# Smaller operand loads and a shared eviction in a talking-heads attention plus two-MoE-layer kernel

## The chip, the cores and the metric

The kernel runs on one core of a Trainium2 chip. The metric is the device time of one execution in microseconds (us), as a median of runs. Differences of under about 0.3% (2.2 us here) count as no change.

## The reference

Two batches, 12 heads, 448 positions, 64 values per head, all float32. Attention mixes its heads twice: the scores before the softmax with `w_pre`, the weights after it with `w_post`.

```python
scores = scale * np.matmul(q, k.transpose(0, 1, 3, 2))
scores = np.einsum('bhij,hg->bgij', scores, w_pre)
scores = scores - np.max(scores, axis=-1, keepdims=True)
attn = np.exp(scores)
attn = attn / (np.sum(attn, axis=-1, keepdims=True) + 1e-09)
attn = np.einsum('bhij,hg->bgij', attn, w_post)
return np.matmul(attn, v)
```

Its output, 896 tokens of 768 values, passes a gated layer (`g = x @ w_gate; x = silu(g) * (x @ w_val) @ w_out`, inner width 1536) and a second one (`h = x @ w_in; x = h * relu6(h + 3) / 6 @ w_out`, inner width 2048).

## The kernel before

The order of all work is written out by hand; nothing is scheduled by a planner. Within an engine instructions run in that order, and so do the DMA issues of a queue (SP's, except a few of ACT's at the start).

Attention works on **tiles** of up to 120 query positions, four per batch (t = 0 to 7), and inside a tile on **chunks** of 10 positions: 12, 12, 12, 9 and 11, 12, 12, 10 chunks, 90 in all. Two chunks are a **pair**, and a pair is one **step** of the main loop at the kernel's end (i = 0 to 44). One step holds, in PE's order:

- `postmix(i)`: 64 small products of the softmax numerators `e` with the scaled weights `wn` into two PSUM tiles `ppost` (two buffers, so both are in use; the next `postmix` has to wait until both are evicted).
- `qk(t, c)`: the scores of one pair of heads for a tile that is needed later, into two PSUM tiles, evicted by `scores_out` (one by DVE, one by ACT) into the score tile `S`. A step holds one of these, steps 0 to 2, 15 and 17 two, and steps 37 to 44 none.
- `premix(i + 2)`: the mixing by `w_pre` of pair i + 2, from the tile `sx`.
- in 21 of the steps `av`: the products with the values of an earlier tile.

DVE takes the row maxima (`row_max`), ACT the exponentials (`exps`), DVE and POOL the weights `wn` (`weights`). `attn_out(i)` evicts the two `ppost` tiles into the tile `at`; before, ACT does both.

Between `qk` and `premix` the scores change their layout, from one head per plane to heads across partitions. That is the work of `relayout(m)`: for each chunk SP issues two DMAs from `S` to `sx`, one of 104 rows (182 KB) and one of 24 rows (42 KB), every row 1792 bytes long. A tile's chunks can only be relaid once all its scores are evicted; that is at the end of steps 2, 8, 14, 18, 24, 30 and 36 for tiles 1 to 7. Six chunks (fewer at step 18) are then issued at once, the others two per step.

On the same SP queue go the loads: query and key tiles of batch 1 (`load_q(1, ..)` and `load_k(1, ..)`, 1350 and 1344 KB, at the end of steps 4 and 5), the values (`load_v`, 1536 KB each: batch 0 ahead of the loop, batch 1 at step 8), and two weight pieces (`fetch`, 768 KB each, at steps 20 and 28). After the loop PE does the two layers without a break.

Of the kernel before, what the change touches and what calls it, by code (L numbers as in the profile page):

```python
# [18 lines left out]
DM = H * D  # L19
HP = H // 2  # L20
# [7 lines left out]
JC = 4  # L28
# [19 lines left out]
def kernel(  # L48
# [14 lines left out]
    nc = tc.nc  # L63
# [31 lines left out]
    qs, ks, vs = {}, {}, {}  # L95
# [5 lines left out]
    def load_q(b, i0, i1):  # L101
        lo, hi = (HP * KI * sum(c for _, _, c in TILES[b][:i]) for i in (i0, i1))
        nc.sync.dma_start(out=qs[b][:, lo:hi], in_=qT[b, :, lo:hi])

    def load_k(b, c0, c1, eng=nc.sync):
        eng.dma_start(out=ks[b][:, c0:c1, :], in_=kT[b, :, c0 * S : c1 * S].rearrange("p (c j) -> p c j", j=S))

    def load_v(b):
        vs[b] = pv.tile([128, JC, H, D], F32, name=f"v{b}", tag="v")
        nc.sync.dma_start(out=vs[b].rearrange("p c h d -> p (c h d)"), in_=vv[b])  # L110

    def load_q0(c0, c1, eng):
        n = TILES[0][0][2] * KI
# [7 lines left out]
    load_k(0, 2, 3)  # L121
    load_k(0, 3, 4, nc.scalar)
    load_k(0, 4, 5)
    load_k(0, 5, 6, nc.scalar)
    W1 = cst.tile([128, 64], F32, name="W1")
    W2 = cst.tile([128, H, KG], F32, name="W2")
    nc.scalar.dma_start(out=W1, in_=w_pre)
    nc.scalar.dma_start(out=W2.rearrange("p g k -> p (g k)"), in_=w_post)
    nc.gpsimd.tensor_scalar(W1, W1, 0.125, 1.0, ALU.mult, ALU.mult)
    load_q(0, 1, 4)  # L130

    Ss = [psc.tile([128, H + 1, S], F32, name=f"S{i}") for i in range(2)]
    for x in Ss:
# [48 lines left out]
    def relayout(m, small=nc.sync):  # L182

        t, c = chunks[m]
        b, i = divmod(t, 4)
        ncc = TILES[b][i][2]  # L190
        i, r = divmod(m, 2)
        if r == 0:
            sx[i] = psx.tile([128, 2, S], F32, name=f"sx{i}", tag="sx")
        rows = stiles[t][c : ncc * KI : ncc, :, :]
        nc.sync.dma_start(out=sx[i][0:104, r, :], in_=rows[:8, :, :])  # L195
        small.dma_start(out=sx[i][104:128, r, :], in_=rows[8:, :H, :])
# [3 lines left out]
    def premix(i):  # L200

        x = sx.pop(i)
        p = [ps.tile([128, 512], F32, name=f"ppre{i}_{a}", tag="ppre", bufs=BUFS["ppre"]) for a in range(2)]
        for r in range(2):
            for a in range(2):
                rows = slice(64 * a, 64 * a + 64)
                nc.tensor.matmul(  # L207
                    p[a][64 * r : 64 * r + 64, :S],
                    lhsT=W1[rows, :],
                    rhs=x[rows, r, :],  # L210
                    start=True,
                    stop=True,
                    tile_position=(64 * a, 64 * r),
                )
        for a in range(2):
            pre[2 * i + a] = p[a]

    def row_max(m):
        nm = pe.tile([128, 1], F32, name=f"nm{m}", tag="nm", bufs=6)
        nc.vector.tensor_reduce(nm, pre[m][:, :S], AX.X, ALU.max, negate=True)  # L220
        tot[m] = nm

    def exps(m):
        e = es[m % 6]
        sm = pe.tile([128, 1], F32, name=f"sm{m}", tag="sm", bufs=6)
        nc.scalar.activation(e[:, :S], pre.pop(m)[:, :S], AF.Exp, bias=tot.pop(m), scale=1.0, accum_out=sm)  # L226
        ew[m] = (e, sm)

    def weights(m):
        sm = ew[m][1]  # L230
        rc = pe.tile([128, 1], F32, name=f"rc{m}", tag="rc", bufs=6)
        nc.vector.tensor_scalar(rc, sm, 1e-9, None, ALU.add)
        nc.vector.reciprocal(rc, rc)  # L233
        wn = pe.tile([128, H, KG], F32, name=f"wn{m}", tag="wn", bufs=6)
        nc.gpsimd.tensor_scalar(wn, W2, rc, 1.0, ALU.mult, ALU.mult)  # L235
        wns[m] = wn

    def postmix(i):
        p = [
            ps.tile([128, 2, JC, H, KG], F32, name=f"ppost{i}_{s}", tag="ppost", bufs=BUFS["ppost"]) for s in range(2)  # L240
        ]
        for r in range(2):
            e, wn = ew.pop(2 * i + r)[0], wns.pop(2 * i + r)
            for b in range(JC):
                for c in range(2):
                    k0 = (2 * b + c) * JB
                    for s in range(2):
                        rows = slice(64 * s, 64 * s + GP)
                        nc.tensor.matmul(  # L249
                            p[s][64 * c : 64 * c + 64, r, b, :, :],  # L250
                            lhsT=e[rows, k0 : k0 + 64],
                            rhs=wn[rows, :, :],
                            start=True,
                            stop=True,
                            tile_position=(64 * s, 64 * c),
                        )
        post[i] = p

    def attn_out(i):
        p = post.pop(i)  # L260
        (t0, c0), (t1, c1) = chunks[2 * i], chunks[2 * i + 1]
        for t, c in ((t0, c0), (t1, c1)):
            if c == 0:
                ats[t] = pat.tile([128, JC, H, 120], F32, name=f"at{t}", tag="at")
        for r in range(2):
            if t0 == t1:
                dst = ats[t0][:, :, :, c0 * KI : (c0 + 2) * KI].rearrange("p b h (a k) -> p a (b h) k", k=KI)
                dst = dst[:, :, :, r * KG : (r + 1) * KG]
            else:
                t, c = chunks[2 * i + r]  # L270
                dst = ats[t][:, :, :, c * KI : (c + 1) * KI].rearrange("p b h (a k) -> p a (b h) k", k=KG)
            nc.scalar.copy(dst, p[r].rearrange("p a b h k -> p a (b h) k"))  # L272

    pavs, stage, xt = {}, {}, {}

# [154 lines left out]
    def halve(j):  # L430
        if j < len(subs):
            kind, idx, k0, kc, _ = subs[j]
            _, y, _ = ys.pop(j)
            pool = pools["wp0" if j < 2 else "wp"]
            whl[j] = split_w(pool, y, kc, f"{kind}{idx}_{k0}")
# [33 lines left out]
    for _ in range(8):  # L469
        relayout(placed, nc.scalar if placed < 4 else nc.sync)  # L470
        placed += 1
    load_v(0)


    extra = {i: {"qk": [], "av": [], "end": []} for i in range(-LOOK, NP)}

    def at_step(i, f, *args, place="end"):
        extra[i][place].append((f, args))

    def run(i, place):  # L480
        for f, args in extra[i][place]:
            f(*args)
# [15 lines left out]
    for t in range(7):  # L498
        begin = (first[t + 1] - 1) // 2 + 1
        end = first[t + 2] // 2 - 1 if t < 6 else NP - 1  # L500
        for c in range(HP):
            i = begin + (c // 2) * (end - begin) // 2
            at_step(i, av, t, c, place="av")
            at_step(i, x_out if t < 6 else x_last, t, c)
        if t < 6:
            step = 1 if t < 4 else 2
            i = split_at.setdefault(t, max(end + 1, split_at.get(t - 1, 0) + 4 // step))
            for part in range(4):
                at_step(i + part // step, x_split, t, part)
    at_step(4, new_qk, 1)  # L510
    at_step(4, load_q, 1, 0, 4)
    at_step(5, load_k, 1, 0, 6)
    at_step(8, load_v, 1)
    for b in range(2):
        at_step(scored[4 * b + 3] + 1, new_x, b)

# [7 lines left out]
    def fill(n):  # L524
        nonlocal fillers
        if fillers is None:
            fillers = first_products()
        for _ in range(n):
            next(fillers, None)

    for i in range(-LOOK, NP):
        if i >= 0:
            postmix(i)
        soft = [2 * (i + 1) + a for a in range(2)] if 0 <= i + 1 < NP else []
        for m in soft:
            exps(m)
        for m in soft[:1]:
            weights(m)
        run(i, "qk")
        for m in soft[1:]:  # L540
            weights(m)
        if i + LOOK < NP:
            premix(i + LOOK)
            for a in range(2):
                row_max(2 * (i + LOOK) + a)
        if i >= 0:
            attn_out(i)
        if i >= NP - 3:
            fill(FILL[i - NP + 3])
        run(i, "av")  # L550
        if i == 41:
            late.close()
            pools["wp0"] = ctx.enter_context(tc.tile_pool(name="wp0", bufs=2, side="right"))
        if i in (42, 43):
            halve(i - 42)
        run(i, "end")
        while placed < NCH and placed // 2 <= i + LOOK + 4 and i >= scored.get(chunks[placed][0], -3):
            relayout(placed)
            placed += 1
# [158 lines left out]
```

## Time and profile before

| | |
|---|---|
| median of 3 runs | 729.32 us (727.85 to 730.26) |
| profiled execution | 731.22 us, of which the span from first to last instruction is 729.4 us |
| mean granted TensorE clock | 0.988 of full speed |
| PE / DVE / ACT / POOL busy | 703.0 / 480.5 / 317.1 / 122.7 us |
| DMA | 86.66 MB, 119 GB/s on average |
| share of the chain that ended last | PE 86%, DMA 8%, ACT 3% |

The busy share of PE (96%) counts overlapped instructions and says little by itself. The chain, the gaps ahead of PE's instructions and the starts of the steps tell more. A row of the timeline reads: start, duration, engine, line, operation, output and inputs, count, and in brackets how long the engine had been idle and who ended that. PE is the matmul, PEld the weight load ahead of it, SPq the issue of a DMA by SP. Instructions on DVE and ACT overlap by some tenths, so the distance between two starts is what an instruction occupies.

### The profile page before, as it was taken

To read this page: it belongs to the slowest core of one execution; us is meant where nothing else is said; L and a number is where in the kernel's file an instruction comes from. 1 tells how busy PE (TensorE), PEld (TensorE's weight loads), DVE (VectorE), ACT (ScalarE), POOL (GpSimd) and SP (SyncE) were. 2 spreads that over 40 slices of the span, in tenths; PEclk is the share of its full clock that TensorE was granted. 3 is DMA by queue.
4 is the path that set the end of the run, shared out by engine and by line. 5 is a ranking of instruction groups with operands and counts; after the bars stand their busy time and mean duration, and the time that the engine had idled before them with its cause. 6 is when DMAs were issued, how large, how long until landed. Compare 5 with 4: busy or idle time off the path is not lost.

```text
span 729.4 us, 16450 instructions
## 1 busy us (share of the span) xinstructions
PE 703.0 (96%) x6864; PEld 580.7 (80%) x6864; DVE 480.5 (66%) x808; ACT 317.1 (43%) x608; POOL 122.7 (17%) x185
## 2 busy tenths in 40 slices
PE   8898989999999999999999999999999999999998
PEld 2354446565668999999999999999999999999997
DVE  2563455576751788888878766657888888665550
ACT  2573466687663443343333333224354453333230
POOL 0110112332151111311211100001323324000000
PEclk9898999999999999999999999999999999999999
DMA  5548322434231233333333423332233232544320
GB/s 208 177 153 258 115 78 100 153 127 162 102 114 73 87 126 101 120 122 106 119 93 124 130 88 102 118 127 87 87 102 116 86 123 81 175 143 137 117 90 26
DMA packets 26462, 86.66 MB, mean 119 GB/s; under 512 B 2708, under 2 KB 16788, under 8 KB 25876
## 3 DMA queue, kind: packets, MB, share of 16 engines
q1 hardware_dynamic: 25420, 84.44, 35.0%
q8 instruction: 54, 0.88, 0.5%
q10 hardware_dynamic: 968, 1.17, 0.5%
q14 instruction: 20, 0.16, 0.1%
HBM read 62.20 MB, written 2.75 MB: 89 GB/s over the span
## 4 chain that ended last, share of the span: by engine, by line
PE 86%; DMA 8%; ACT 3%; SPq 2%; issue 1%; POOL 0%; DVE 0%; ACTq 0%
PE pi L383 16%; PE pp L383 16%; PE po L383 12%; PE pg L383 12%; PE pv L383 12%; PE ppost L249 5%; PE pav L284 5%; DMA sx<-S 5%; PE pqk L162 4%; PE ppre L207 3%; ACT at L272 2%; DMA v<-in_v_dram 1%; ACT S L178 1%; PE p L383 1%; SPq L195 1%; DMA W<-in_w_pre_dram 1%
## 5 line engine op out<-in xcount | busy, mean ns | idle before, releaser
L383 PE MATMUL pp<-g,hp 128*128 128x448 f32 x384 | 109.1, 365 | 0.0
L383 PE MATMUL po<-u,ho 128*128 128x448 f32 x288 | 81.7, 364 | 0.0
L249 PEld LDWEIGHTS ppost<-wn,e 60*64 60x64 f32 x2880 | 53.8, 138 | 34.7 <-issue 23.2
L383 PEld LDWEIGHTS pp<-g,hp 128*128 128x128 f32 x384 | 71.9, 187 | 5.8
L249 PE MATMUL ppost<-wn,e 60*64 60x60 f32 x2880 | 62.4, 226 | 11.9 <-issue 5.6
L207 PE MATMUL ppre<-sx,W 64*64 64x448 f32 x360 | 65.0, 564 | 5.7 <-DMA sx<-S 5.7
L383 PE MATMUL pi<-x2h,li 128*128 128x448 f32 x192 | 70.2, 366 | 0.0
L579 POOL TENSOR_TENSOR g<-rl,g 128x448 fp32r<-128x448 f32 x32 | 41.5, 1318 | 169.0 <-ACT g L578 169.0
L383 PE MATMUL pi<-x2l,hi 128*128 128x448 f32 x192 | 70.0, 364 | 0.0
L383 PE MATMUL pi<-x2h,hi 128*128 128x448 f32 x192 | 69.9, 364 | 0.0
L383 PE MATMUL pp<-g,lp 128*128 128x448 f32 x192 | 69.3, 361 | 0.0
L220 DVE TENSOR_REDUCE nm<-ppre 128x1 f32<-128x448 f32 x90 | 52.5, 617 | 23.8 <-PE ppre L207 23.1
L226 ACT ACTIVATE e<-ppre,nm 128x448 f32<-128x448 f32 x90 | 56.5, 633 | 22.4 <-DVE nm L220 20.9
L178 DVE COPY S<-pqk 120x448 f32<-120x448 f32 (+3 forms) x48 | 30.0, 624 | 51.5 <-PE pqk L162 51.2
L579 POOL TENSOR_TENSOR u<-sg,u 128x448 fp32r<-128x448 f32 x24 | 32.7, 1380 | 151.3 <-ACT u L578 151.3
L383 PEld LDWEIGHTS po<-u,ho 128*128 128x128 f32 x288 | 54.1, 188 | 3.8
L162 PE MATMUL pqk<-k,q 64*64 64x448 f32 (+4 forms) x384 | 53.2, 555 | 3.4 <-ACT S L178 3.4
L235 POOL TENSOR_SCALAR wn<-W,rc 128x60 f32<-128x60 f32 x90 | 28.2, 314 | 163.1 <-DVE rc L233 101.7
L272 ACT COPY at<-ppost 128x480 f32<-128x480 f32 x90 | 52.8, 647 | 3.7 <-PE ppost L249 3.7
L383 PE MATMUL po<-u,lo 128*128 128x448 f32 x144 | 52.3, 363 | 0.0
L284 PEld LDWEIGHTS pav<-at,v 128*64 128x64 f32 x768 | 38.3, 140 | 16.3 <-ACT S L178 9.9
L383 PE MATMUL pv<-xl,hv 128*128 128x448 f32 x138 | 50.5, 366 | 0.0
(103 smaller groups left out, 1362.1 us busy)
## 6 DMA issues: line engine op xcount, KB each, us to landing
sx<-S SPq DMA_DIRECT2D x90, 182.0 KB
ri<-in_moe_w_in_dram SPq DMA_DIRECT2D x16, 768.0 KB
rg<-in_moe_w_gate_dram SPq DMA_DIRECT2D x12, 768.0 KB
rv<-in_moe_w_val_dram SPq DMA_DIRECT2D x12, 768.0 KB
ro<-in_moe_w_out_dram SPq DMA_DIRECT2D x12, 768.0 KB
rp<-in_moe_w_out_dram SPq DMA_DIRECT2D x12, 640.0 KB
rp<-in_moe_w_out_dram SPq DMA_DIRECT2D x6, 768.0 KB
sx<-S SPq DMA_DIRECT2D x86, 42.0 KB
```

Source lines behind the costliest of these rows:

```text
L162: nc.tensor.matmul(p[e][lo:hi, :S], lhsT=qs[b][r, base + lo : base + hi], rhs=ks[b][r, c, :], start=True, stop=True, tile_position=(64 * e ...
L178: copy(stiles[t][:n, h, :], pqk.pop((t, h))[:n, :S])
L195: nc.sync.dma_start(out=sx[i][0:104, r, :], in_=rows[:8, :, :])
L207: nc.tensor.matmul(p[a][64 * r : 64 * r + 64, :S], lhsT=W1[rows, :], rhs=x[rows, r, :], start=True, stop=True, tile_position=(64 * a, 64 * r),
L220: nc.vector.tensor_reduce(nm, pre[m][:, :S], AX.X, ALU.max, negate=True)
L226: nc.scalar.activation(e[:, :S], pre.pop(m)[:, :S], AF.Exp, bias=tot.pop(m), scale=1.0, accum_out=sm)
L235: nc.gpsimd.tensor_scalar(wn, W2, rc, 1.0, ALU.mult, ALU.mult)
L249: nc.tensor.matmul(p[s][64 * c : 64 * c + 64, r, b, :, :], lhsT=e[rows, k0 : k0 + 64], rhs=wn[rows, :, :], start=True, stop=True, tile_pos ...
L272: nc.scalar.copy(dst, p[r].rearrange("p a b h k -> p a (b h) k"))
L284: nc.tensor.matmul(p[64 * e : 64 * e + 64, :n], lhsT=vs[b][:, jc, h, :], rhs=ats[t][:, jc, h, :n], start=jc == 0, stop=jc == JC - 1, tile_ ...
L383: nc.tensor.matmul(p[:, :S], lhsT=wt[:, kk, :], rhs=xx, start=start, stop=stop)
L579: eng.tensor_tensor(to[1], src, to[0].bitcast(F32), ALU.subtract)
```

## The change

1. Loads of attention operands become small pieces. Values: four pieces of 384 KB per batch, one a step, for batch 0 at steps 1 to 4, for batch 1 at steps 17 to 20. Keys of batch 1: six pieces of 224 KB at steps 5 to 10. Queries of batch 1: four pieces of one tile each (300 to 360 KB) at steps 11 to 14. Queries of batch 0: tile 1 at the start as before, tiles 2 and 3 at steps 0 and 1. The last key piece of batch 0 goes from ACT's to SP's queue.
2. `attn_out` stands ahead of `weights`, `qk` and `row_max` in a step instead of behind them, and its first half goes to DVE, the second to ACT.

The order of PE's and of POOL's instructions stays the same.

```diff
+    def load_v(b, j):
+        nc.sync.dma_start(
+            out=vs[b][:, j].rearrange("p h d -> p (h d)"), in_=vv[b, :, j * DM : (j + 1) * DM]
+        )
...
-    load_k(0, 5, 6, nc.scalar)
+    load_k(0, 5, 6)
...
-    load_q(0, 1, 4)
+    load_q(0, 1, 2)
...
-            nc.scalar.copy(dst, p[r].rearrange("p a b h k -> p a (b h) k"))
+            copy = nc.scalar.copy if r else nc.vector.tensor_copy
+            copy(dst, p[r].rearrange("p a b h k -> p a (b h) k"))
...
-    load_v(0)
+    new_v(0)
...
-    at_step(4, new_qk, 1)
-    at_step(4, load_q, 1, 0, 4)
-    at_step(5, load_k, 1, 0, 6)
-    at_step(8, load_v, 1)
+
+    for n in range(2):
+        at_step(n, load_q, 0, 2 + n, 3 + n)
+    for j in range(JC):
+        at_step(1 + j, load_v, 0, j)
+    at_step(5, new_qk, 1)
+    for n in range(HP):
+        at_step(5 + n, load_k, 1, n, n + 1)
+    for n in range(4):
+        at_step(11 + n, load_q, 1, n, n + 1)
+    at_step(16, new_v, 1)
+    for j in range(JC):
+        at_step(17 + j, load_v, 1, j)
...
+        if i >= 0:
+            attn_out(i)
         for m in soft[:1]:
             weights(m)
         run(i, "qk")
...
-        if i >= 0:
-            attn_out(i)
```

On SP's queue, behind the first six chunks of tile 1 (the rows start with the last of them; `sx` is a relayout, `q`, `k`, `v` are loads), there stood in steps 3 to 5:

```order
L195 DMA sx_502<-S_108 104x1x448
L196 DMA sx_502<-S_108 24x1x448
L195 DMA sx_575<-S_108 104x1x448
L196 DMA sx_575<-S_108 24x1x448
L195 DMA sx_575<-S_108 104x1x448
L196 DMA sx_575<-S_108 24x1x448
L103 DMA q_648<-in_q_dram 128x2700
L195 DMA sx_651<-S_108 104x1x448
L196 DMA sx_651<-S_108 24x1x448
L195 DMA sx_651<-S_108 104x1x448
L196 DMA sx_651<-S_108 24x1x448
L106 DMA k_649<-in_k_dram 128x2688
```

In the changed kernel the same place on SP's queue reads:

```order
L199 DMA sx_505<-S_108 104x1x448
L200 DMA sx_505<-S_108 24x1x448
L112 DMA v_217<-in_v_dram 128x768
L199 DMA sx_579<-S_108 104x1x448
L200 DMA sx_579<-S_108 24x1x448
L199 DMA sx_579<-S_108 104x1x448
L200 DMA sx_579<-S_108 24x1x448
L112 DMA v_217<-in_v_dram 128x768
L199 DMA sx_653<-S_108 104x1x448
L200 DMA sx_653<-S_108 24x1x448
L199 DMA sx_653<-S_108 104x1x448
L200 DMA sx_653<-S_108 24x1x448
```

The two large loads between the pairs have gone, and the last two pieces of batch 0's values stand there in their place, behind four pairs of relayouts.

On DVE the step with the scores of head pair 3 of tile 2 (step 6; `rc` belongs to `weights`, `nm` is `row_max`) read:

```order
L232 TENSOR_SCALAR rc_768<-sm_764 128x1
L233 RECIPROCAL rc_768<-rc_768 128x1
L178 COPY S_107<-pqk_3_0_773 120x448
L232 TENSOR_SCALAR rc_781<-sm_766 128x1
L233 RECIPROCAL rc_781<-rc_781 128x1
L220 TENSOR_REDUCE nm_792<-ppre_0_786 128x1
L220 TENSOR_REDUCE nm_794<-ppre_1_787 128x1
```

On DVE the same step of the changed kernel reads:

```order
L277 COPY at_772<-ppost_0_734 128x2x48x5
L236 TENSOR_SCALAR rc_775<-sm_768 128x1
L237 RECIPROCAL rc_775<-rc_775 128x1
L182 COPY S_107<-pqk_3_0_780 120x448
L236 TENSOR_SCALAR rc_788<-sm_770 128x1
L237 RECIPROCAL rc_788<-rc_788 128x1
L224 TENSOR_REDUCE nm_799<-ppre_0_793 128x1
L224 TENSOR_REDUCE nm_801<-ppre_1_794 128x1
```

One eviction has come to DVE, ahead of everything else in the step. On ACT the step with the scores of head pair 5 of that tile read, exponentials first:

```order
L226 ACTIVATE e_111,sm_922<-ppre_0_876,nm_882 128x448
L226 ACTIVATE e_112,sm_924<-ppre_1_877,nm_884 128x448
L178 COPY S_107<-pqk_5_1_932 120x448
L272 COPY at_796<-ppost_0_888 128x2x48x5
L272 COPY at_796<-ppost_1_889 128x2x48x5
```

On ACT it now reads:

```order
L230 ACTIVATE e_111,sm_928<-ppre_0_883,nm_889 128x448
L230 ACTIVATE e_112,sm_930<-ppre_1_884,nm_891 128x448
L277 COPY at_772<-ppost_1_895 128x2x48x5
L182 COPY S_107<-pqk_5_1_940 120x448
```

The eviction left to ACT now stands ahead of the score eviction.

## Rows read from the trace of the kernel before

**Rows 1.** The chain of waits: start us, us, what (where the two layers begin).

```profile
237.19 3.84 PE pg L383 x18
```

**Rows 2.** The timeline of PE: steps 8, 12, 19 and 20.

```profile
58.36 1.09 PE L249 MATMUL ppost<-wn,e 60*64 60x60 f32 x59 [0.19 <-ACT at L272]
...
88.82 1.16 PE L249 MATMUL ppost<-wn,e 60*64 60x60 f32 x64
...
123.58 1.16 PE L249 MATMUL ppost<-wn,e 60*64 60x60 f32 x64
...
126.17 1.86 PE L284 MATMUL pav<-at,v 128*64 128x120 f32 x32
127.96 1.16 PE L249 MATMUL ppost<-wn,e 60*64 60x60 f32 x64
128.94 0.93 PE L162 MATMUL pqk<-k,q 64*64 64x448 f32 x8
129.69 0.93 PE L207 MATMUL ppre<-sx,W 64*64 64x448 f32 x8
...
131.62 1.09 PE L249 MATMUL ppost<-wn,e 60*64 60x60 f32 x59 [0.19 <-ACT at L272]
```

**Rows 3.** The timeline of the other engines at the end of step 20.

```profile
129.93 0.62 DVE L178 COPY S<-pqk 120x448 f32<-120x448 f32 x1 [1.31 <-PE pqk L162]
...
130.40 1.18 ACT L272 COPY at<-ppost 128x480 f32<-128x480 f32 x2
130.47 0.14 DVE L232 TENSOR_SCALAR rc<-sm 128x1 f32<-128x1 f32 x1
...
130.73 1.16 DVE L220 TENSOR_REDUCE nm<-ppre 128x1 f32<-128x448 f32 x2
130.98 0.31 POOL L235 TENSOR_SCALAR wn<-W,rc 128x60 f32<-128x60 f32 x1 [1.88 <-DVE rc L233]
```

**Rows 4.** The timeline of PE's weight loads: waits for relaid pairs.

```profile
44.44 0.19 PEld L207 LDWEIGHTS ppre<-sx,W 64*64 64x64 f32 x2 [0.22 <-DMA sx<-S]
...
52.01 0.19 PEld L207 LDWEIGHTS ppre<-sx,W 64*64 64x64 f32 x2 [0.49 <-DMA sx<-S]
...
177.67 0.19 PEld L207 LDWEIGHTS ppre<-sx,W 64*64 64x64 f32 x2 [0.69 <-DMA sx<-S]
...
181.28 0.19 PEld L207 LDWEIGHTS ppre<-sx,W 64*64 64x64 f32 x2 [0.63 <-DMA sx<-S]
...
201.22 0.19 PEld L207 LDWEIGHTS ppre<-sx,W 64*64 64x64 f32 x2 [0.68 <-DMA sx<-S]
...
205.10 0.19 PEld L207 LDWEIGHTS ppre<-sx,W 64*64 64x64 f32 x2 [0.72 <-DMA sx<-S]
...
216.34 0.19 PEld L207 LDWEIGHTS ppre<-sx,W 64*64 64x64 f32 x2 [0.67 <-DMA sx<-S]
```

**Rows 5.** The timeline of SP: issues at the pauses of the queue.

```profile
37.57 0.69 SPq L195 DMA_DIRECT2D sx<-S  x1
...
92.02 0.65 SPq L196 DMA_DIRECT2D sx<-S  x1
102.19 0.69 SPq L195 DMA_DIRECT2D sx<-S  x1
...
116.19 0.67 SPq L196 DMA_DIRECT2D sx<-S  x1
121.85 0.69 SPq L195 DMA_DIRECT2D sx<-S  x1
...
194.52 0.70 SPq L195 DMA_DIRECT2D sx<-S  x1
```

**Rows 6.** Stretches: us, busy PE PEld DVE ACT POOL, clock, DMA share, GB/s.

```profile
5.00:10.00 5.00, 4.96 (x48) 1.63 (x40) 3.06 (x5) 3.87 (x6) 0.00 (x0) 1.00 0.95 353
54.00:56.00 2.00, 2.00 (x84) 1.66 (x84) 0.78 (x4) 0.46 (x2) 0.31 (x1) 1.00 1.02 313
66.00:68.00 2.00, 2.00 (x13) 1.02 (x12) 1.25 (x2) 0.92 (x3) 0.00 (x0) 0.50 1.03 375
```

More of the change, by code (lines that the diff above doesn't have):

```diff
@@ L106, in load_k, with new_v @@
         eng.dma_start(out=ks[b][:, c0:c1, :], in_=kT[b, :, c0 * S : c1 * S].rearrange("p (c j) -> p c j", j=S))
-    def load_v(b):
+    def new_v(b):
         vs[b] = pv.tile([128, JC, H, D], F32, name=f"v{b}", tag="v")
-        nc.sync.dma_start(out=vs[b].rearrange("p c h d -> p (c h d)"), in_=vv[b])
+    def load_v(b, j):
+        nc.sync.dma_start(
+            out=vs[b][:, j].rearrange("p h d -> p (h d)"), in_=vv[b, :, j * DM : (j + 1) * DM]
+        )
     def load_q0(c0, c1, eng):
```

## The prediction, made before the change was run

> **What bounds the kernel now.** I read the chain of waits first, then PE's timeline step by step, then what PE's weight loads waited for, then SP's queue. The chain shows that the two layers begin at 237.19 us [rows 1], and from there hardly anything but PE is on it. Nothing in that stretch changes, so the forecast is about the first 237 us.
>
> The steps there are of two kinds. A step with value products (call it A) takes 127.96 - 123.58 = 4.38 us, of which these products are 127.96 - 126.17 = 1.79 us, and PE waits for nothing [rows 2]. A step without them (N) takes 131.62 - 127.96 = 3.66 us, though its work on PE is only 4.38 - 1.79 = 2.59 us: the next `postmix` waits for ACT, which evicts both `ppost` tiles last in its step, from 130.40 to 131.58 us [rows 2, 3].
>
> The second limit is the path of the relaid chunks; call it the conveyor. SP issues in order and the copies land in order. How fast they land shows where PE waits for pair after pair: the last copies of two pairs lie 52.01 - 44.44 = 7.57 us apart, those of neighbours 181.28 - 177.67 = 3.61 and 205.10 - 201.22 = 3.88 us [rows 4]. That is 15.06 us for four pairs, 3.76 us a pair and 1.88 us a chunk. SP issued the nine chunks of tile 3, 18 copies, from 102.19 to 116.19 us, about 1.6 us a chunk [rows 5]: the copies are moved more slowly than they are issued.
>
> So how full is the conveyor? From the first issue for tile 1 at 37.57 us to the last landing at 216.34 us [rows 4, 5] there are 178.8 us and 78 chunks: 78 x 1.88 = 146.6 us. Through the same queue go queries, keys and values of batch 1 and two weight pieces, 1350 + 1344 + 1536 + 2 x 768 = 5766 KB by the tiles' shapes; at 313 GB/s, the rate while two of them pass [rows 6], that is 18.9 us. The lead of the first pair is 44.44 - 37.57 - 3.76 = 3.1 us [rows 4, 5]. That leaves 178.8 - 146.6 - 18.9 - 3.1 = 10.2 us in which the conveyor stands still. They are found in SP's pauses: 92.02 to 102.19 and 116.19 to 121.85 us are two of them, the last ends at 194.52 us [rows 5], and of each some 4 us go to copies that are still landing. So this kernel alternates: first PE waits for loads and copies, then the conveyor waits for scores.
>
> A page of the Trainium skill, *DMA: Bandwidth & Descriptors*, section on why a DMA increments its semaphore by 16, says that such a DMA runs on as many of the 16 engines as divide the slowest dimension of both sides: by it the large copy (8 groups of 13 rows into 104) would use 8 engines, the small one (2 groups of 12 into 24) two of these. Two engines would then carry 25 of the 1792-byte rows of every chunk, 44.8 KB, which would explain a slow conveyor at a low mean share. At the page's 27 GiB/s an engine that would be, as an estimate, 1.5 us a chunk, and SP's issue would set the pace; the landings give 1.88, and the measurement decides.
>
> **The change, part by part.** *The eviction.* One `ppost` copy goes to DVE (480 elements; the `S` copy of 448 occupies 130.47 - 129.93 = 0.54 us [rows 3], so 0.58 us). The trace shows no DVE copy that writes runs of five elements; the bounds are 0.58 and twice that, 1.16 us, and I take 0.58, since the nearest row also reads PSUM. In an N step the chain becomes: `postmix` 128.94 - 127.96 = 0.98 us; the wake-up 129.93 - 129.69 = 0.24; the eviction 0.58; the first weights 130.73 - 130.47 = 0.26; the `S` copy 0.54; the second weights to the end of `wn` 131.29 - 130.47 = 0.82. That is 3.42 us, and the second half of the next `postmix` (0.49 us in) needs it, so N takes 2.9 to 3.0 us instead of 3.66 [rows 2, 3]. DVE's own load in it is 0.58 + 0.26 + 0.54 + 0.26 + 1.06 = 2.7 us, less than that. A stays at 4.38, because PE was not waiting there. Over 16 such N steps this is about 11 us of PE time, if PE sets the pace.
>
> *The large loads.* In before, queries, keys and values of batch 1 stand between the pairs of tile 1 and 2; from step 8 to step 12 PE needs 88.82 - 58.36 = 30.5 us [rows 2] for what is 4.4 + 3.7 + 3.7 + 5.4 = 17.2 us of work (tile 3's score products are slower). Spread out, these 4230 KB take the same 13.8 us of the conveyor; they are only no longer in one place. Two things get worse. First, two pieces of batch 0's values, 768 KB or 2.5 us, now go through the conveyor behind 37.57 us, ahead of which all of them went before. Second, the last of them stands behind four pairs of tile 1 on SP's queue, and step 6 needs it: 36.6 (start, below) + 3.1 + 4 x 3.76 + 2.5 = 57 us, while PE would be ready at about 51.5. PE will stand there for some 5 us and leave step 6 at about 58 us, 3 us later than before. The conveyor runs on meanwhile, so this costs the end little.
>
> *The start.* Less is loaded ahead of the first relayout, and steps 0 to 2, with two score products, each lose part of the wait for ACT: I take 1 us in all at the first issue for tile 1 (bounds 0 and 2.5), so 36.6 us. The key piece that changes queues lies ahead of the work that needs it: nothing.
>
> *The sum.* With PE faster in N steps and no block of loads, PE keeps ahead of the conveyor nearly everywhere, and the conveyor sets the end of attention. Between the issue points of two tiles it needs, with the pieces (0.7 us for a key piece, 1.25 for a value piece, 1.1 for a query piece): steps 3 to 8 28 us, 9 to 14 28.5, 15 to 18 19.4, 19 to 24 25.7 (with a weight piece), 25 to 30 25.1 (another), 31 to 36 22.6, and 18.8 for the last ten chunks. PE needs about 18, 27.4, 19.1, 23, 21.6 and 22.3 us for the six spans. The sum is 168 us; with 36.6 + 3.1 and 1.5 us for the start of tile 2's copies, which the wait in step 6 delays, the last pair lands at 209.3 us instead of 216.34. The gain is 7 us: 1.0 + 10.2 - 1.5 - 2.5. The 21 us from there to the layers stay. In the profiled execution's own time, 731.2 us, that is 724.2; it lies 1.9 us above the median of the runs, 729.3, so against these I forecast 722 us.
>
> Bounds: with 1.81 or 1.94 us a chunk (the closest and the widest pair) the idle time of before is 15.7 or 5.5 us and the gain 12.5 or 2.5 us, so 717 to 727.
>
> **The rivals.** *The conveyor is not the limit* (its pace follows SP's issues, and these follow PE). Then the steps' savings count in full: 11 us from N steps, 13 from steps 8 to 11, less 4 for the wait in step 6: 20 us, 709 us. For it: SP's pauses show that it had time. Against it: the three equal intervals, at times far apart.
>
> *PE falls behind after step 6.* After PE had waited for copies about 60 us, the granted clock from 66 to 68 us was 0.50, the lower of the two levels, 1.2 GHz [rows 6]; the wait in step 6 may do the same. If the next steps run so, tile 2's scores come 3 to 5 us later, the conveyor idles that long, and 3 us of gain remain: 726 us.
>
> *Small pieces hold the conveyor longer than their bytes* (slower). Sixteen pieces stand between relayouts. A copy of only 42 KB lands some 0.9 us after its large neighbour; were each piece to cost that much more than its bytes, it would be 14 us, and 736 us; from 0.45 us a piece on, the change loses. For it: these copies show that a small DMA is not cheap. Against it: from 5 to 10 us, where pieces of 224 KB and less were under way beside one large one, 353 GB/s were moved [rows 6]. The page named above, section Bandwidth, states the rule for this side: transfers should be batched to at least 1 MiB, with some 2 us fixed per DMA. If that were serial it would be, as an estimate, 32 us; the row speaks against it, since the fixed parts overlapped there.
>
> *The gains cancel* (a slower DVE eviction at 1.16 us makes N 3.5 us, and the conveyor idles as before): 729 us.
>
> **How the numbers follow.** Chances: the forecast 0.60, conveyor not the limit 0.13, PE behind 0.13, pieces slow 0.07, gains cancel 0.07. A measurement of this kernel tells 0.3%, 2.2 us, from no change, so faster means under 727.1. Faster: 0.59 of the forecast's, 0.13, and 0.08 of the third, 0.80; within 0.3%: 0.12; slower 0.08. The range of 8 in 10 runs from 712 to 728: it takes in the forecast's 717 to 727, the third case and the slower part of the second; what lies outside is most of 709, and 736.
>
> **What would show it.** Right: the layers begin at about 230 us; landings at 3.7 to 3.9 us a pair nearly without a pause from tile 1 on; PE waiting for `sx` in more steps than before, above all about steps 24 and 32; N steps of 2.9 to 3.0 us where no copy is awaited; no wait for ACT ahead of `postmix`; a wait of about 5 us for `v` in step 6. Wrong: a layers' begin at 217 us, or pairs that land faster than every 3.5 us, would show that the conveyor was no limit; windows with loads at well under 300 GB/s and pairs 5 us apart, that pieces are slow.

## The result, and the profile after

The changed kernel takes 721.98 us in the median (721.87 to 723.24), the kernel before beside it 728.59; the ratio is 0.991, with an interval of 0.989 to 0.994. A second set of runs gave 723.45 us and the same ratio, 0.991 [0.989, 0.993]. The forecast was 722 us, with 0.80 for faster.

| | before | after |
|---|---|---|
| profiled execution / span | 731.22 / 729.4 us | 721.89 / 720.0 us |
| the layers begin | 237.19 us | 227.07 us |
| first issue for tile 1 | 37.57 us | 35.43 us |
| last pair lands | 216.34 us | 207.11 us |
| conveyor stands still between the two | 7.8 us | 0.7 us |
| DVE / ACT busy | 480.5 / 317.1 us | 504.4 / 296.1 us |
| chain: PE / DMA / ACT / DVE | 86 / 8 / 3 / 0% | 88 / 4 / 3 / 3% |

The line on the standstill is counted from the packets' start times and durations: the stretches of over 0.3 us between those two times in which no packet of SP's queue was moving. In before it is the next three windows; the columns end with PE's clock, DMA's busy share and GB/s.

```profile
98.70:103.53 4.83, 4.81 (x102) 2.67 (x104) 2.66 (x8) 3.26 (x8) 0.63 (x2) 1.00 0.01 3
120.96:123.18 2.22, 2.22 (x40) 1.52 (x34) 1.99 (x6) 1.98 (x4) 0.74 (x2) 1.00 0.04 8
195.12:195.85 0.73, 0.73 (x19) 0.73 (x16) 0.73 (x3) 0.73 (x2) 0.10 (x1) 1.00 0.00 0
```

After, one is left. The second window here is the clock behind the wait for `v` in step 6.

```profile
65.20:65.93 0.73, 0.73 (x20) 0.73 (x16) 0.73 (x2) 0.65 (x3) 0.00 (x0) 1.00 0.00 0
56.18:59.59 3.41, 3.41 (x76) 3.10 (x78) 0.56 (x2) 0.00 (x0) 0.00 (x0) 0.50 0.45 147
```

So the account is short. The conveyor was moving for 178.8 - 7.8 = 171.0 us before and 171.7 - 0.7 = 171.0 us after. It began 2.1 us earlier and lost 7.1 us less; together that is the 9.2 us by which the last pair lands earlier. The layers begin 10.1 us earlier. The profile of the second set scatters about this: 1.8 us of standstill, the last pair at 207.66 us, the layers at 227.56 us.

The chain of waits after, where the layers begin (compare [rows 1]):

```profile
222.88 4.19 PE pav L289 x96
227.07 3.88 PE pg L388 x18
```

PE's timeline: the wait in step 6, then steps 20 and 21 (compare [rows 2]).

```profile
51.32 0.84 PE L289 MATMUL pav<-at,v 128*64 128x120 f32 x12
56.00 2.14 PE L289 MATMUL pav<-at,v 128*64 128x120 f32 x20 [3.85 <-DMA v<-in_v_dram]
58.07 1.23 PE L253 MATMUL ppost<-wn,e 60*64 60x60 f32 x36
...
117.38 1.16 PE L253 MATMUL ppost<-wn,e 60*64 60x60 f32 x64
118.36 0.93 PE L166 MATMUL pqk<-k,q 64*64 64x448 f32 x8
119.11 0.93 PE L211 MATMUL ppre<-sx,W 64*64 64x448 f32 x8
120.05 1.47 PE L253 MATMUL ppost<-wn,e 60*64 60x60 f32 x64
...
123.22 1.86 PE L289 MATMUL pav<-at,v 128*64 128x120 f32 x32 [0.19 <-ACT S L182]
125.01 0.28 PE L253 MATMUL ppost<-wn,e 60*64 60x60 f32 x4
```

Counted from the first product of a `postmix` to that of the next, the N step is 120.05 - 117.38 = 2.67 us, and the A step behind it 125.01 - 120.05 = 4.96 us. In before, [rows 2] has only the 59 products of step 21 that had to wait; the first ones of that step, and of the step behind it, stand here:

```profile
131.14 0.29 PE L249 MATMUL ppost<-wn,e 60*64 60x60 f32 x2 [0.52 <-issue]
...
136.00 1.16 PE L249 MATMUL ppost<-wn,e 60*64 60x60 f32 x64
```

So, by the same count, the N step was 131.14 - 127.96 = 3.18 us and the A step 136.00 - 131.14 = 4.86 us: the one has become 0.51 us shorter, the other 0.10 us longer. Rows of the other engines from that A step show what it waits for:

```profile
120.82 0.56 PEld L253 LDWEIGHTS ppost<-wn,e 60*64 60x64 f32 x32 [0.22 <-POOL wn L239]
...
121.57 0.67 DVE L277 COPY at<-ppost 128x480 f32<-128x480 f32 x1 [0.23 <-PE ppost L253]
122.16 0.14 DVE L236 TENSOR_SCALAR rc<-sm 128x1 f32<-128x1 f32 x1
...
122.14 0.64 ACT L277 COPY at<-ppost 128x480 f32<-128x480 f32 x1
...
122.61 0.55 ACT L182 COPY S<-pqk 120x448 f32<-120x448 f32 x1
```

The second half of `postmix` waits for `wn` until 120.82 us, 3.44 us behind the `postmix` before; in before the held products waited for ACT until 131.62 us, 3.66 us behind it. So there is still a wait, for another engine and a little shorter. And ACT's copy of the scores now stands behind its eviction, so `av` waits for the PSUM tile that this copy frees.

The waits for relaid pairs are more in number (22 rows against 16 between 37 and 220 us, 18 in the second profile), but not in total time (20.0 us against 20.3 over the whole kernel; compare [rows 4]). Here are the last copies of tile 1's first three pairs, waits about steps 24 and 32, and the last one.

```profile
42.64 0.19 PEld L211 LDWEIGHTS ppre<-sx,W 64*64 64x64 f32 x2 [0.71 <-DMA sx<-S]
...
46.51 0.19 PEld L211 LDWEIGHTS ppre<-sx,W 64*64 64x64 f32 x2 [0.68 <-DMA sx<-S]
...
50.42 0.19 PEld L211 LDWEIGHTS ppre<-sx,W 64*64 64x64 f32 x2 [0.68 <-DMA sx<-S]
...
134.11 0.19 PEld L211 LDWEIGHTS ppre<-sx,W 64*64 64x64 f32 x2 [0.67 <-DMA sx<-S]
135.07 0.19 PEld L211 LDWEIGHTS ppre<-sx,W 64*64 64x64 f32 x2 [0.77 <-DMA sx<-S]
135.90 0.19 PEld L211 LDWEIGHTS ppre<-sx,W 64*64 64x64 f32 x2 [0.64 <-DMA sx<-S]
...
168.54 0.19 PEld L211 LDWEIGHTS ppre<-sx,W 64*64 64x64 f32 x2 [0.81 <-DMA sx<-S]
...
207.11 0.19 PEld L211 LDWEIGHTS ppre<-sx,W 64*64 64x64 f32 x2 [0.67 <-DMA sx<-S]
```

What the conveyor does inside a chunk shows in short windows of a stretch in which SP issues without a break:

```profile
163.10:163.60 0.50, 0.50 (x12) 0.27 (x8) 0.50 (x2) 0.50 (x1) 0.00 (x0) 1.00 0.54 212
163.90:164.25 0.35, 0.35 (x8) 0.00 (x0) 0.16 (x1) 0.35 (x1) 0.23 (x1) 1.00 0.08 21
164.50:165.10 0.60, 0.58 (x32) 0.44 (x32) 0.56 (x4) 0.00 (x0) 0.00 (x0) 1.00 0.52 200
165.40:165.55 0.15, 0.04 (x4) 0.04 (x4) 0.15 (x2) 0.00 (x0) 0.15 (x2) 1.00 0.15 60
```

DMA's share swings between a half and about a tenth: while the 104-row copy runs some 8 of the 16 engines are busy, while the 24-row copy runs about 2. Two windows of before, in which nothing but relaid rows is under way, show it more clearly:

```profile
181.80:182.70 0.90, 0.90 (x13) 0.53 (x13) 0.70 (x2) 0.68 (x2) 0.00 (x0) 1.00 0.51 197
182.70:183.62 0.92, 0.92 (x24) 0.92 (x22) 0.48 (x2) 0.82 (x4) 0.00 (x0) 1.00 0.15 57
```

By the packets' times mostly 8 rows are under way at once in the first window and 2 in the second, and a row takes 0.074 us. So the 104 rows are 13 in turn and the 24 rows 12: 25 x 0.074 = 1.85 us, close to the 1.88 us a chunk of the landings.

The rule of the Trainium skill that the prediction named (*DMA: Bandwidth & Descriptors*, why a DMA increments its semaphore by 16) makes it 8 and 2 engines, shares of 0.50 and 0.125, and says that they are the lowest-numbered ones, so that the two copies share two engines. The trace agrees on the shares; it doesn't show which engines they are.

### The profile page after: what moved, and what is told of

It is laid out like the page before. It is cut to its first block, busy times and chain, and to the rows that moved or that the text cites. A ratio compares the mean times of both kernels' runs of the same rounds, so it can differ in the third digit from the quotient of the medians.

```text
span 720.0 us, 16436 instructions
## 1 busy us (share of the span) xinstructions
PE 698.4 (97%) x6864; PEld 575.1 (80%) x6864; DVE 504.4 (70%) x853; ACT 296.1 (41%) x563; POOL 122.4 (17%) x185
## 4 chain that ended last, share of the span: by engine, by line
PE 88%; DMA 4%; ACT 3%; DVE 3%; issue 1%; POOL 0%; SPq 0%; ACTq 0%; POOLq 0%
PE pi L388 16%; PE pp L388 16%; PE po L388 12%; PE pg L388 12%; PE pv L388 12%; PE pav L289 6%; PE ppost L253 5%; PE ppre L211 4%; PE pqk L166 4%; DMA sx<-S 2%; ACT e L230 1%; DMA v<-in_v_dram 1%; PE p L388 1%; DVE S L182 1%; DMA k<-in_k_dram 1%
## 5 line engine op out<-in xcount | busy, mean ns | idle before, releaser
L253 PEld LDWEIGHTS ppost<-wn,e 60*64 60x64 f32 x2880 | 51.7, 136 | 23.2 <-POOL wn L239 15.6
L253 PE MATMUL ppost<-wn,e 60*64 60x60 f32 x2880 | 58.7, 223 | 4.5 <-POOL wn L239 3.3
L166 PE MATMUL pqk<-k,q 64*64 64x448 f32 (+4 forms) x384 | 51.5, 545 | 4.8 <-ACT S L182 4.3
L388 PE MATMUL pg<-xh,hg 128*128 128x448 f32 x138 | 50.6, 367 | 0.0
L388 PE MATMUL pg<-xl,hg 128*128 128x448 f32 x138 | 50.6, 367 | 0.0
```

Source lines behind the costliest of these rows:

```text
L166: nc.tensor.matmul(p[e][lo:hi, :S], lhsT=qs[b][r, base + lo : base + hi], rhs=ks[b][r, c, :], start=True, stop=True, tile_position=(64 * e ...
L253: nc.tensor.matmul(p[s][64 * c : 64 * c + 64, r, b, :, :], lhsT=e[rows, k0 : k0 + 64], rhs=wn[rows, :, :], start=True, stop=True, tile_pos ...
L388: nc.tensor.matmul(p[:, :S], lhsT=wt[:, kk, :], rhs=xx, start=start, stop=stop)
```

## The experiments

Twelve runs; ratios are to the kernel before beside them, with their intervals.

**Each part alone.** The eviction on the loads of before, and the loads with the evictions of before (the two parts of the diff, unedited).

> The kernel before with the eviction alone changed (one half of `attn_out` on DVE, both issued ahead of the weights); its loads stay in large blocks. Theory of the forecast (the conveyor sets the end of attention): N steps take 2.7 to 3.0 us as in the changed kernel, but what they save is mostly waited away for `sx`; the block of loads still holds tile 2's copies, so the layers begin 2 to 5 us before 237.2 and the time is 724 to 727 us against 729. Rival (PE's steps set the end): 16 N steps save about 0.7 us each, 11 us, so about 718 us.

> The kernel before with the loads alone changed (small pieces, one a step); both evictions stay on ACT, last in the step. Theory of the forecast: N steps stay at 3.66 us, PE waits less for `sx` in steps 8 to 11 and some 4 us for `v` in step 6; PE is then slower than the conveyor in many steps, whose pauses stay: the layers begin 2 to 5 us earlier, 724 to 727 us. If the two parts were independent, the two gains would add up to the 7 to 10 us of the whole change. Rival (PE's steps set the end): steps 8 to 11 save 13 us less 4 for `v`: 720 us. Rival (small pieces hold the conveyor): 730 us or more.

The eviction alone: 725.67 us, 0.994 [0.992, 0.996]; the layers begin at 232.4 us, and the conveyor stands still for 6.4 us. The loads alone: 729.78 us, 1.000 [0.998, 1.002]; 235.4 us, 4.5 us. The eviction did what was expected. The loads were worth nothing, less than expected, and the two gains, 4 and 0 us, don't add up to the 7 us of the whole. The account of the conveyor, counted as above, shows where they went:

| us | first issue for tile 1 | standstill | moving | last pair lands |
|---|---|---|---|---|
| before | 37.57 | 7.8 | 171.0 | 216.34 |
| eviction alone | 37.70 | 6.4 | 168.4 | 212.49 |
| loads alone | 37.11 | 4.5 | 172.9 | 214.50 |
| both | 35.43 | 0.7 | 171.0 | 207.11 |
| both, second profile | 35.40 | 1.8 | 170.5 | 207.66 |

Most of the standstill goes only with both. I read it so: with slow steps the scores of a tile come late wherever the loads stand, and with the block of loads PE waits behind it however fast its steps are. The small pieces make the conveyor move for 1.9 us longer with the evictions of before and 2.1 to 2.6 us longer with the shared one; the 768 KB of batch 0's values that now pass it would be 2.5 us by the prediction's own rate. The eviction makes it move for 1.9 to 2.6 us less; the runs don't show why. By its time alone, the kernel with the loads also fits the rival in which small pieces hold the conveyor (730 us or more); by this account they hold it for about what their added bytes would take.

**The wait for `v`.** In the changed kernel, batch 0's pieces ahead of the loop:

```diff
-        at_step(1 + j, load_v, 0, j)
+        load_v(0, j)
```

> The changed kernel with the four value pieces of batch 0 issued ahead of the loop, before any copy of tile 1. Theory of the forecast (the wait for `v` in step 6 costs the end little, because the conveyor runs on behind it): PE no longer waits in step 6, tile 1's first copy is issued some 2 us later, and the time is 721 to 723 us, no change from 722. Rival (PE's delay in step 6 is carried to the end, through the scores of tile 2 that come late): the layers begin 3 to 4 us earlier, 718 to 719 us.

> The changed kernel with batch 0's values issued ahead of the loop, once more, for a second profile. In the first, the profiled execution (721.9 us) was the longest of five and its layers began at 227.1 us as in the changed kernel; the other four took 718.2 to 719.5 us. If the wait in step 6 costs the end 3 us, the time is again 718 to 720 us, and a profile of such an execution shows the layers at about 224 us; if it costs nothing, the time is 721 to 723 us.

719.36 us, 0.985 [0.983, 0.987], and 719.86 us, 0.987 [0.983, 0.991]: 2.6 us below the first set of the changed kernel and 3.6 us below the second, about as the rival said. The profiles don't show how. In both the profiled execution was the longest of its set (721.9 and 721.2 us), the layers begin at 227.2 and 226.4 us, and the conveyor never stands still, having moved for 170.5 and 171.0 us. In the second profile another wait stands in the place of the one removed: the queries of tile 2 now come behind the values.

```profile
40.82 0.98 PE L166 MATMUL pqk<-k,q 64*64 64x448 f32 x8 [2.61 <-DMA q<-in_q_dram]
...
226.44 0.47 PE L388 MATMUL pg<-xh,hg 128*128 128x448 f32 x1
```

What the shorter executions did otherwise stays open.

**The conveyor made cheap.** The 24-row copies left out, and with them the last two queries of each chunk.

```diff
+            sx[i] = sxs[i % 5]
...
-        small.dma_start(out=sx[i][104:128, r, :], in_=rows[8:, :H, :])
```

> The changed kernel without the 24-row copies: rows 104 to 127 of every relaid chunk hold zeros or older rows, so the last two queries of each chunk are not computed; five fixed buffers, cleared once, stand for the five rotating ones. All the work of PE, DVE and ACT stays. In the trace of the changed kernel DMA's busy share alternates between about half (the 104-row copy) and a fifth to a quarter (the 24-row copy), each for some 0.9 us. Theory of the forecast (the conveyor sets the end of attention): a chunk takes 1.0 us or SP's issue, 0.8 us, instead of 1.88; PE waits for `sx` no more, and the layers begin where PE's own steps let them: by the forecast's figure for that case, 709 to 714 us. Rival (the conveyor had room, PE's steps and the points at which scores are ready set the end): 720 to 722 us.

701.88 us, 0.961 [0.959, 0.963]; the layers begin at 207.4 us. That is 20 us less than the changed kernel, with all the work of the other engines still there, so the conveyor was the limit, and removing it is worth more than the 709 us that the prediction had for that case. From 40 us on PE waits for `sx` four times, and the conveyor stands still for 40 us, with windows like this one:

```profile
159.53:170.79 11.26, 10.97 (x272) 6.93 (x264) 10.82 (x31) 6.46 (x15) 1.89 (x6) 1.00 0.01 4
```

**Scores one step earlier.**

```diff
-        end = first[t] // 2 - LOOK - 2
+        end = first[t] // 2 - LOOK - (3 if t > 1 else 2)
```

> The changed kernel with the score products of tiles 2 to 7 ending one step earlier, so that SP may issue each tile's first copies about 3 us earlier. SP pauses in the changed kernel before the first copy of tiles 2 to 7, from 3.6 to 4.7 us in five of six cases. First reading, the one by which the prediction counted idle time (a pause of SP is, beyond some 4 us of copies still landing, lost to the conveyor, and lost time of the conveyor is lost at the end): nothing is left to win but the part of each pause beyond 4 us, 2 us together, so 720 to 722 us. Rival (the pauses themselves hold the end, because PE waits for each tile's first pair): 5 x 2 to 3 us, about 709 to 712 us. Slower than 723 us would show that the extra score product in a step costs PE more than it gives.

721.23 us, 0.988 [0.986, 0.991], 2 us below the changed kernel's 723.45 on the same chip, with intervals that overlap; the conveyor never stands still. The first reading holds: a pause of SP isn't a pause of the conveyor, which has a backlog to work off. (By the trace of the changed kernel four of SP's pauses are 3.6 to 4.7 us long and one 2.5 us.)

**Another cut of the chunk.** The same rows of scores, but 120 and 4 instead of 104 and 24; and the same with the values first, beside the changed kernel itself.

```diff
-        rows = stiles[t][c : ncc * KI : ncc, :, :]
-        nc.sync.dma_start(out=sx[i][0:104, r, :], in_=rows[:8, :, :])
-        small.dma_start(out=sx[i][104:128, r, :], in_=rows[8:, :H, :])
+        rows = stiles[t][c : ncc * KI : ncc, :H, :]
+        nc.sync.dma_start(out=sx[i][0:120, r, :], in_=rows)
+        small.dma_start(out=sx[i][120:124, r, :], in_=rows[KG : KG + 1, :4, :])
```

> The changed kernel with the relaid chunk cut in another way: one copy of 120 rows (ten queries by twelve heads, without the plane of zeros) and one of 4 rows (heads 0 to 3 of the sixth query, which the upper half of PE's rows needs), instead of 104 and 24 rows; the weights' rows are placed to fit, and the score mixing reads 60 rows of each half instead of 64. The same two DMAs a chunk on the same queue, nearly the same bytes (217 KB instead of 224). If the conveyor's pace is the time that the two copies' rows take one after another, about 0.9 us for each in the changed kernel, the 120-row copy takes about 0.9 us again and the 4-row copy at most 0.3; then SP's issue (0.74 us a DMA, 1.48 a chunk) sets the pace instead of 1.88, PE waits little for `sx`, and the time is 703 to 709 us, near the 702 us of the kernel without the 24-row copies. Rival (the pace is set by bytes, or by a fixed time for each DMA): no change, 720 to 723 us.

> The 120-row cut together with batch 0's values issued ahead of the loop. If the conveyor no longer limits, the wait for `v` in step 6 (4 us in the changed kernel) counts in full unless the values come earlier: with them first, 1 to 4 us less than the 120-row cut alone, 701 to 706 us. If the conveyor still limits, as much as the values first gave alone: 0 to 3 us less than the 120-row cut alone.

> The changed kernel once more, unedited, on the chip of the kernels beside it, so that these can be compared with it directly: 722 us, 0.991 of the kernel before.

711.27 us, 0.975 [0.973, 0.977]; with the values first 706.01 us, 0.968 [0.966, 0.970]; the changed kernel 723.45 us. The new cut is 12 us faster with the same number of DMAs and nearly the same bytes, so bytes or a fixed time for each DMA were not the pace; it missed its 703 to 709 us by 2.3 us. The values first then gave 5.3 us, more than the 1 to 4 expected. The pace is now SP's issue. The timeline of SP with the new cut:

```profile
155.41 0.80 SPq L199 DMA_DIRECT2D sx<-S  x1
156.25 0.62 SPq L200 DMA_DIRECT2D sx<-S  x1
156.93 0.80 SPq L199 DMA_DIRECT2D sx<-S  x1
157.78 0.62 SPq L200 DMA_DIRECT2D sx<-S  x1
```

One chunk every 156.93 - 155.41 = 1.52 us, where it was 1.88; SP issues without a break, and in each chunk here no packet moves for some 0.4 us. In the middle of a 120-row copy the share, 0.66, is that of some 10 engines. By the rule of the Trainium skill named above it would be ten too (ten source queries into 120 rows).

```profile
155.50:156.00 0.50, 0.50 (x9) 0.15 (x4) 0.47 (x3) 0.38 (x2) 0.00 (x0) 1.00 0.66 254
```

**The two parts, with the conveyor out of the way.** The last kernel with the evictions of before (first diff; their place too), and the new cut with the shared eviction on the loads of before (second diff).

```diff
-            copy = nc.scalar.copy if r else nc.vector.tensor_copy
-            copy(dst, p[r].rearrange("p a b h k -> p a (b h) k"))
+            nc.scalar.copy(dst, p[r].rearrange("p a b h k -> p a (b h) k"))
```

```diff
+    load_v(0)
...
+    at_step(4, load_q, 1, 0, 4)
+    at_step(5, load_k, 1, 0, 6)
+    at_step(8, load_v, 1)
```

> The kernel with the 120-row cut and the values first, but with the evictions of the kernel before: both on ACT, last in the step. Theory (the conveyor took away most of what the eviction saved): with the conveyor free, PE's steps set the end, the 16 N steps are 0.7 to 1.0 us longer each, and the time is 11 to 16 us above the 706 us of the kernel with the shared eviction: 717 to 722 us. Rival (the shared eviction is worth the 4 us that it gave alone, with or without the conveyor): about 710 us.

> The kernel with the 120-row cut and the shared eviction, but with the loads of the kernel before: batch 0 loaded whole ahead of the loop, batch 1 in three blocks in steps 4, 5 and 8. Theory (blocks of loads cost what they hold up, wherever copies are awaited behind them): the block of 4230 KB takes 13.8 us at 313 GB/s, of which the conveyor's lead, now 0.3 to 0.4 us a chunk larger, covers a part; PE waits some 4 to 8 us for tile 2's first pairs, 710 to 714 us. Rival (with the faster cut the conveyor catches up before PE needs the pairs): 705 to 708 us.

713.52 us, 0.978 [0.974, 0.983], and 709.92 us, 0.974 [0.970, 0.978], against 706.01. So the eviction is worth 7.5 us here, neither the 11 to 16 of the theory nor the 4 of the rival; on the changed kernel's loads it was worth 6 to 8 as well (729.8 against 722.0 to 723.5). So beside small loads the conveyor didn't take its saving: the saving is smaller than I had it. Step N and the A step behind it take 131.62 + 4.38 - 127.96 = 8.04 us in before [rows 2] and 125.01 - 117.38 = 7.63 us after, 0.41 us; were each of 16 pairs of steps to save as much, it would be 6.6 us in all, an estimate from this one pair. The loads are worth 3.9 us, a little less than expected, but only together with the values first, which the 706.01 us have and the change doesn't. The kernel with the new cut and the loads as the change has them takes 711.27 us, and the loads of before are no worse than these (709.92). With the loads in a block PE still waits for tile 2's first pairs:

```profile
55.21 0.20 PEld L207 LDWEIGHTS ppre<-sx,W 60*64 60x64 f32 x4 [2.59 <-DMA sx<-S]
56.46 0.19 PEld L207 LDWEIGHTS ppre<-sx,W 60*64 60x64 f32 x4 [1.06 <-DMA sx<-S]
...
67.82 0.20 PEld L207 LDWEIGHTS ppre<-sx,W 60*64 60x64 f32 x4 [1.42 <-DMA sx<-S]
```

**The place of the eviction.** Shared, but last in the step as before.

```diff
-        if i >= 0:
-            attn_out(i)
         for m in soft[:1]:
             weights(m)
...
+        if i >= 0:
+            attn_out(i)
         if i >= NP - 3:
```

> The changed kernel with `attn_out` put back to its old place, last in the step, but still shared by DVE and ACT. Theory (what the eviction edit saves comes from both, sharing and place): DVE reaches its half only behind the `S` copy, the second weights and the two row maxima, so it ends at about the time at which ACT ended both, N steps stay at 3.3 to 3.7 us, and the time is that of the loads alone, 728 to 730 us. Rival (sharing alone halves the eviction): ACT and DVE end 0.5 us earlier, N steps take 3.0 to 3.2 us, 724 to 726 us.

743.63 us, 1.020 [1.015, 1.025]: 15.6 us slower than the kernel before beside it, and 14 us slower than the same loads with both evictions on ACT (729.78 us), which neither theory allowed for. The timeline of an N step (132.24 us is its `postmix`; 136.90 us is the part of the next one that had to wait):

```profile
132.24 1.23 PE L253 MATMUL ppost<-wn,e 60*64 60x60 f32 x61
...
134.80 0.64 ACT L277 COPY at<-ppost 128x480 f32<-128x480 f32 x1
...
135.13 1.14 DVE L224 TENSOR_REDUCE nm<-ppre 128x1 f32<-128x448 f32 x2
...
136.18 0.66 DVE L277 COPY at<-ppost 128x480 f32<-128x480 f32 x1
...
136.76 0.14 DVE L236 TENSOR_SCALAR rc<-sm 128x1 f32<-128x1 f32 x1
136.90 1.09 PE L253 MATMUL ppost<-wn,e 60*64 60x60 f32 x59 [1.06 <-DVE rc L236]
```

On DVE the eviction stands behind both row maxima, 1.14 us, and ends at 136.18 + 0.66 = 136.84 us, when ACT has long ended its half (135.44 us); PE goes on 0.06 us later. Read alone, the wait is put down to the `rc` that was in progress; by the clock it is the eviction. Up to these products it is 136.90 - 132.24 = 4.66 us, where it was 3.66 in before. So the place alone decides whether sharing helps or harms: the earlier place isn't a detail of the change but its condition.

## Why the prediction was right

**The limit.** That the conveyor sets the end of attention was right, and is shown by the kernel without the 24-row copies (20 us less) and by the new cut (12 us less). Its pace was right too: the first pairs of tile 1 land 3.87 and 3.91 us apart, and the waits gather where they were expected, about steps 24 and 32. The rival in which the conveyor is not the limit is refuted.

**The sum.** It read 1.0 + 10.2 - 1.5 - 2.5 = 7.2 us at the last landing; measured are 2.1 + 7.1 = 9.2. That 722 us came out is in part luck, for its terms were less good than their sum:
- The start was mis-sized: 2.1 us earlier instead of 1.0 (in the bounds of 0 to 2.5).
- The standstill of before was 7.8 us, not 10.2.
- The 2.5 us for the values that now pass the conveyor don't show between before and after, 171.0 us of moving each. With equal evictions the loads did add 1.9 to 2.6 us, and the eviction took as much off, a gain that the sum doesn't have. Whether it is the values that added it stays open: with the values first the conveyor moved for 170.5 and 171.0 us.
- The 1.5 us at the start of tile 2's copies was 0.7, 1.3 in the second profile.

The layers then begin at 227.07 us, not at about 230; the 21 us between the last landing and the layers became 20.0. In the profiled execution's own time I forecast 724.2 us, and it took 721.89; the medians moved by less, 6.6 us. So the time was right to a tenth of a per cent partly because the profiled execution of before, at 731.2 us, lay above its median.

**The N steps.** The chain that I put at 3.42 us, from one `postmix` to the second half of the next, took 120.82 - 117.38 = 3.44 us, and DVE's eviction occupied 122.16 - 121.57 = 0.59 us, as the lower bound of 0.58 said. The half standing 0.49 us inside, that is an N step of 2.95 us, as forecast. What failed is the saving, on two counts. First, the 3.66 us of before ran to the 59 products that waited; two stood ahead of them, from 131.14 us, so by first products an N step was 3.18 us and is 2.67, a gain of 0.51. Second, "A stays at 4.38": counted as the forecast did, A takes 7.63 - 2.95 = 4.68 us behind an N step. Of the 0.30 us more, 0.19 are the wait for the score tile, which the eviction brought ahead of ACT's `S` copy; I had counted what the early eviction frees, but not what it delays. So this pair of steps saves 0.41 us instead of some 0.7, and all of them, by the estimate above, 6.6 us instead of 11; the runs with the new cut measured 7.5.

**Step 6.** The wait for `v` came as forecast: PE stood from 52.2 to 56.0 us and began step 7 at 58.07 us (forecast 58). So did the lower clock of the second rival: 0.50 of full speed, 1.2 GHz, from 56.18 to 59.59 us, after PE had stood still. It didn't decide, because the conveyor ran on. But that this costs the end little was too low: with the values first the median is some 3 us shorter.

**Small pieces.** No sign of a cost beyond bytes: for sixteen more DMAs, and 768 KB more behind the first issue, the conveyor moves for 1.9 to 2.6 us longer, where the bytes alone make 2.5. The 2 us fixed per DMA that the prediction quotes from the Trainium skill (*DMA: Bandwidth & Descriptors*) stand there in the section on the anatomy of a DMA, as a fit for DMAs issued from GpSimd; the pieces here are issued by SP, and nothing near 32 us shows.

## What to carry to other kernels

When several things take turns in being late, a part of a change can be worth nothing alone and 2 to 4 us beside the other; try them together before one is given up, and once more when the limit has moved, for with the new cut the same loads were worth nothing again until the values came first. Before an instruction is given to an engine with room, read what stands ahead of it there: on the same loads the same shared eviction gained some 7 us in one place and lost 14 in another. And for a stream of copies look at how many DMA engines a copy keeps busy, not at its bytes: cutting 104 + 24 rows into 120 + 4 gained more than the whole change did, and the two together (706.0 us) are the fastest version here that computes everything.

## What was not expected of the hardware

A pause of SP's queue is no pause of the transfers: SP paused for 4.7 us ahead of 64.56 us and ahead of 185.11 us, and only 0.7 us of standstill is left in the whole stretch (1.8 in the second profile). A chunk of 224 KB took 1.88 us as 104 + 24 rows, and 217 KB took at most 1.52 us as 120 + 4, then limited by the issue of two DMAs, 0.80 and 0.62 us. In the first cut 25 rows came one after another, 0.074 us each.
